# Spreading weight conversions by single steps, and moving the lead's low parts to GpSimd

## The chip, the cores and the metric

The kernel runs on one core of a Trainium2 chip. Its time is the device time of one execution in microseconds (us). TensorE (PE) multiplies matrices, VectorE (DVE), ScalarE (ACT) and GpSimd (POOL) work elementwise, and SyncE (SP) issues the transfers. Each engine takes its instructions in the order of its own queue; across engines an instruction waits on semaphores.

## The reference

```
scores = scale * q @ k^T                      # 4 batches, 8 heads, 768 tokens, 64 per head
keep   = (column < n_global) | (0 <= row - column < n_local)      # 8 and 96
a      = softmax(where(keep, scores - slope[h] * distance, -1e9))
x      = (a @ v), heads joined                # 3072 tokens x 512
h      = x @ w_in                             # 512 x 2048
out    = max(0.01 * h, h) @ w_out             # 2048 x 512
```

The weights come to the chip as float64.

## The kernel before

**Precision.** Each operand of the FFN is held as a high part in the format fp32r and a low part that is the rest, and each product is made of three matmuls: high by high, low by high, high by low (lines 797 to 799 and 818 to 820).

**Weights.** `w_in` and `w_out` come in 32 pieces; piece 2f is block f of `w_in`, piece 2f + 1 block f of `w_out`. A piece is loaded as float64 bits by the SP queue (`load_piece`, line 98, three pieces ahead, four buffers) and turned into its two parts by `split_float64` in five steps: scale (ACT, L560), shift (two DVE instructions, L563 and L565), low (DVE, L569), high (ACT, the cast L573) and rest (DVE, L576, which writes the low part). The steps depend on each other in that order, so that the piece goes back and forth between ACT and DVE. `conversion(p)` gives the first three steps to its caller and leaves high and rest in the list `due`.

**Attention.** It goes by units of one block of 128 tokens and four heads, 48 in all. `event(t)` issues the scores of unit t, the transposes of unit t - 1 (L274) and the product with v of unit t - 2 (L314, L326), and the softmax of unit t between: bias and minimum on DVE (L195), exponentials on ACT (L210), sums and reciprocals on DVE (L230, L231), and for the units below 14 a diagonal matrix `dg` on POOL (L245), by which the transposing matmul scales the rows. The high and low parts of x follow (L339 on ACT, L343 on DVE). From unit 22 on, `visit` does two units at a time.

**FFN.** Tokens go in eight chunks of 384. For each chunk there are 16 blocks f: `hidden` (called ffn1 in the text) makes block f of the hidden layer in one PSUM bank, `ps_h`; ACT copies it out (L801), DVE applies the leaky ReLU (L802), ACT casts the high part gh (L807) and DVE makes the low part gl (L808). `project` (ffn2) adds its product with `w_out` to three PSUM banks, `ps_o`, one for each 128 tokens.

**Order.** The lead is the first eight events; in events 1 to 7 pieces 0 to 6 are converted, with the steps of event t's piece between its softmax and high and rest of the piece before. After that the work goes by slots j (the loop at line 508): blocks 0 to 6 of chunk 0 are slots 0 to 6, all 16 blocks of chunk 1 are slots 7 to 22, the other blocks of chunk 0 are slots 23 to 31, and the later chunks follow. A slot issues its events (`ev_at`), then ffn1 of slot j, then ffn2 of slot j - 1. Within ffn1, `end` is called between L802 and L807 and `more` after L808. `conv_at` says which pieces a slot converts: the first in the slot's event, if there is one, the others in `more`; `end` issues what is in `due`. At slot 7, ffn2 of slot 6 ends with three ACT copies of the unfinished sums of chunk 0 (`kept`, L458), which free `ps_o` for chunk 1; a finished chunk's sums are copied by ACT, DVE, ACT (L471, L469) and written out.

Instructions that go through `pin` keep the order in which they are written on their engine. That holds for everything named up to slot 22; from slot 23 on the events below unit 22 and the slot work are not pinned, and the copies of finished chunks never are, so that the framework's planner places them.

Of the kernel before, what the change touches and what calls it, by code (L numbers as in the profile page):

```python
# [10 lines left out]
F32 = mybir.dt.float32  # L11
# [5 lines left out]
ALU = mybir.AluOpType  # L17
# [13 lines left out]
LEAD_CONV = 7  # L31
# [3 lines left out]
def spread(items, slots):  # L35

    out = {}
    for n, x in enumerate(items):
        out.setdefault(slots[n * len(slots) // len(items)], []).append(x)
    return out  # L40
# [7 lines left out]
def fast_path(ctx, tc, qp, kp, vp, wi, wo, nvec, weights, nmall, out, B, H, S):  # L48
    nc = tc.nc
# [3 lines left out]
    NF = wi.shape[0]  # L53
# [9 lines left out]
    raw = ctx.enter_context(tc.tile_pool(name="raw", bufs=2))  # L63
    att = ctx.enter_context(tc.tile_pool(name="att", bufs=2))
# [20 lines left out]
    staged = {}  # L85
# [8 lines left out]
    def load_piece(p):  # L94
        if p < len(pieces):
            m, f = pieces[p]
            t = raw.tile([P, NK * P], I64, tag="stage", name="wst", bufs=STAGES)
            pin(nc.sync.dma_start(out=t, in_=(wi, wo)[m][f].rearrange("p a b -> p (a b)")))
            staged[p] = t

    due = []

    def conversion(p):

        m, f = pieces[p]
        dh, dl = ((wih[:, :, f * P:(f + 1) * P], wil[:, :, f * P:(f + 1) * P]), (woh[:, f, :], wol[:, f, :]))[m]
        for n in range(p + 2 + (p > LEAD_CONV - 2), p + 3 + (p > LEAD_CONV - 3)):
            load_piece(n)
        scale, shift, low, *parts = split_float64(tc, pin, att, staged.pop(p), dh, dl)
        due.extend(parts)  # L110
        return scale, shift, low

# [232 lines left out]
    def event(t, conv=()):  # L345

        now, mid, old = t < NUNIT, t - 1 in units, t - 2 in units
        if t < LEAD + 2:

            av = (ps_lead if t % 2 else ps_x).tile([P, 2, 512], F32, tag="ps_av", name="ps_sc")  # L350
            scores(t, av)
            if mid and t <= LEAD:
                transposes(t - 1)
            if old:
                ov = ps_lead.tile([P, 2, 512], F32, tag="ps_ov", name="ps_ov")
                attn_v(t - 2, ov)
            if t > LEAD:

                transposes(t - 1)
        else:  # L360

            ov = av = ps_x.tile([P, 2, 512], F32, tag="ps_av", name="ps_av")
            attn_v(t - 2, ov)
            if now:
                scores(t, av)
            if mid:
                transposes(t - 1)
            high_x(t - 2, ov)
        if t + 2 < NUNIT:
            load_qk(t + 2)  # L370
        if t == 0:
            load_piece(1)
        ends = due[:]
        due.clear()
        if ends:
            ends[0]()
        scale, shift, low = conversion(conv[0]) if conv else [lambda: None] * 3
        if t + 1 < NUNIT:
            load_v(t + 1)
        scale()  # L380
        if now:
            biased(t, av)
            if t == LEAD + 1:
                high_x(t - 2, ov)
            if mid and t >= LEAD + 2:

                keep_pt(t - 1)
            exps(t)
        if t > LEAD:
            low_x(t - 2, ov)  # L390
        if ends:
            ends[1]()
        shift()
        if now:
            sums(t)
        low()
        if old and t <= LEAD:
            high_x(t - 2, ov)
        if mid and t < LEAD + 2:
            keep_pt(t - 1)  # L400
        if old and t <= LEAD:
            low_x(t - 2, ov)

    def visit(t, behind):

        ts = (t, t + 1)
        avs = [ps_x.tile([P, 2, 512], F32, tag=tag, name="ps_v") for tag in ("ps_av", "ps_t")]
        for u, av in zip(ts, avs):
            attn_v(u - 2, av)
        if t < NUNIT:  # L410
            for u, av in zip(ts, avs):
                scores(u, av)
        for u in ts:
            if u + 2 < NUNIT:
                load_qk(u + 2)
            if u + 1 < NUNIT:
                load_v(u + 1)
        for u, av in zip(ts, avs):
            high_x(u - 2, av)
        if t < NUNIT:  # L420
            biased(t, avs[0])
            exps(t)
            biased(t + 1, avs[1])
        for u, av in zip(ts, avs):
            low_x(u - 2, av)
        if t < NUNIT:
            behind.extend([lambda: exps(t + 1, [0]), lambda: (exps(t + 1, [1]), sums(t)), lambda: None, lambda: sums(t + 1)])


    half = 7  # L430
# [44 lines left out]
            eng.dma_start(out=out[r0:r0 + P, :], in_=ob)  # L475


    conv_at = {0: [7], 1: [8], 2: [9], 3: [10, 11], 4: [12], 5: [13], 6: [14]}
    conv_at.update(spread(range(15, 19), range(half, half + 4)))
    conv_at.update(spread(range(19, 2 * NF), range(half + 4, half + NF - 1)))  # L480
    ev_at = {}
    for c in range(1, NCHUNK):
        events = range(NU * first_step[c] + 2, NU * first_step[c + 1] + 2)
        slots = (range(1, half) if c == 1 else [23, 25, 26, 28, 29, 31] if c == 2 else [33, 35, 37, 40, 42, 44] if c == 3
                 else range((c - 1) * NF, c * NF - 2))
        if c > 3:

            events, slots = events[::2], [(c - 1) * NF + s for s in (2, 7, 12)]
        elif c == 3:
            events, slots = [20, 21, 22, 24], [2 * NF + s for s in (0, 3, 7, 12)]  # L490
        ev_at.update(spread(events, slots))

    for t in range(2):
# [14 lines left out]
    for j in range(len(order) + 1):  # L508
        pinned[0] = j < half + NF or bool(behind) or any(t >= PAIRS for t in ev_at.get(j, ()))
        conv = list(conv_at.get(j, ()))  # L510
        for t in ev_at.get(j, ()):
            if t >= PAIRS:
                visit(t, behind)
            else:
                event(t, conv[:1])
            conv = conv[1:]

        def end():
            for step in due:
                step()  # L520
            due.clear()
            if behind:
                behind.pop(0)()

        def more():
            if behind:
                behind.pop(0)()
            for n, p in enumerate(conv):
                if n:
                    end()  # L530
                for step in conversion(p):
                    step()
        if j == half:

            scale_bias(tc, tabs[:, 1], nbw, H, 2)
            scale_bias(tc, tabs[:, 0, HALF:], nb0, H, 2)
        if j == len(order) - NF // 4:
            band_holds(tc, fl, nvec, nmall)
        if j == len(order) - NF // 4 + 1:
            band_holds_everywhere(tc, fl, ps_x.tile([P, 2, 512], F32, tag="ps_t", name="ps_f")[0:1, 0, 0:1], flag)  # L540
        if j < len(order):
            ffn1(j, end, more)
        if j:
            ffn2(j - 1)
    return flags[0]


def split_float64(tc, pin, pool, raw, dh, dl):

    nc = tc.nc
    w2 = raw.bitcast(I32).rearrange("p (n two) -> p n two", two=2)
    lo, hi = w2[:, :, 0], w2[:, :, 1]
    w = pool.tile([P, lo.shape[1]], F32, tag="work", name="w32", bufs=2)
    wb = w.bitcast(I32)
    w3 = w.rearrange("p (a b) -> p a b", a=dh.shape[1]) if len(dh.shape) == 3 else w

    def scale():
        pin(nc.scalar.activation(out=w, in_=hi.bitcast(F32), func=AF.Copy, scale=2.0 ** -112))  # L560

    def shift():
        pin(nc.vector.tensor_scalar(out=wb, in0=wb, scalar1=3, scalar2=0x7FFFFFF8,  # L563
                                    op0=ALU.logical_shift_left, op1=ALU.bitwise_and))
        pin(nc.vector.scalar_tensor_tensor(out=wb, in0=hi, scalar=-0x80000000, in1=wb,  # L565
                                           op0=ALU.bitwise_and, op1=ALU.bitwise_or))

    def low():
        pin(nc.vector.scalar_tensor_tensor(out=wb, in0=lo, scalar=29, in1=wb,  # L569
                                           op0=ALU.logical_shift_right, op1=ALU.bitwise_or))  # L570

    def high():
        pin(nc.scalar.copy(out=dh, in_=w3))  # L573

    def rest():
        pin(nc.vector.tensor_tensor(out=dl, in0=w3, in1=dh.bitcast(F32), op=ALU.subtract))  # L576

    return scale, shift, low, high, rest

# [50 lines left out]
def scale_bias(tc, tab, nb, H, parts):  # L630
    nc = tc.nc
    for h in range(H):
        nc_scale(nc, nc.gpsimd, nb, tab, h, H, parts)
# [263 lines left out]
```

## Time and profile before

| | |
|---|---|
| median of 3 runs | 651.44 us (650.1 to 651.76) |
| profiled execution | 651.29 us, its span 649.8 us |
| PE / DVE / ACT / POOL busy | 627.9 / 375.3 / 282.2 / 22.1 us |
| mean granted TensorE clock | 0.997 |
| first FFN matmul | 37.84 us after the span's start |

A row of a timeline gives start, duration, engine, line, operation, output and inputs, shapes, count, and in brackets how long the engine stood before it and what released it. A row of waits gives the waiting engine and line, the releaser, and the wait in all, how many times, and the longest. Rows of PE with one matmul are pipelined: their starts tell more than their durations.

### The profile page before, as it was taken

What the parts mean: (1) busy time and instruction counts of PE and PEld (TensorE: products, weight loads), DVE (VectorE), ACT (ScalarE), POOL (GpSimd) and SP (SyncE); (2) the same over time, 40 slices, a digit from 0 to 9 for tenths busy, and PEclk for the clock granted to TensorE, in tenths of its full rate; (3) what the DMA queues carried; (4) which work ended last, traced back from release to release, by engine and by line L of the source; (5) the groups of instructions that cost most, each with busy time, mean ns of one, the idle gap of its engine ahead of it and who ended that gap; (6) DMA issues with size and microseconds to landing.
All of it is one profiled execution on the core that took longest, in us unless ns stands there. A gap on an engine that the chain in (4) does not pass through costs nothing.

```text
span 649.8 us, 14540 instructions
## 1 busy us (share of the span) xinstructions
PE 627.9 (97%) x5740; PEld 555.6 (86%) x5740; DVE 375.3 (58%) x1121; ACT 282.2 (43%) x796; POOL 22.1 (3%) x48
## 2 busy tenths in 40 slices
PE   6689999999999999999999999999999999999996
PEld 4478898887888888988989888989889889999985
DVE  5989978895667454553654645545645547232222
ACT  6887855554444343352442442443433524232222
POOL 3212400000000000000000000000000000000000
PEclk9899999999999999999999999999999999999999
DMA  8996634423667433343534443334343432010001
GB/s 268 321 329 202 201 128 144 145 66 121 218 204 234 135 86 115 117 155 115 174 127 153 151 116 114 131 129 152 124 132 137 159 114 98 2 49 0 2 2 52
DMA packets 55163, 88.06 MB, mean 136 GB/s; under 512 B 9776, under 2 KB 30256, under 8 KB 55088
## 3 DMA queue, kind: packets, MB, share of 16 engines
q1 hardware_dynamic: 54944, 86.79, 40.8%
q8 instruction: 47, 0.77, 0.5%
q10 hardware_dynamic: 144, 0.26, 0.1%
q14 instruction: 28, 0.23, 0.1%
HBM read 67.90 MB, written 19.14 MB: 134 GB/s over the span
## 4 chain that ended last, share of the span: by engine, by line
PE 88%; DVE 5%; ACT 4%; DMA 1%; issue 1%; POOL 0%; SPq 0%; POOLq 0%; DVEq 0%; ACTq 0%
PE ps_h L797 14%; PE ps_h L799 13%; PE ps_h L798 13%; PE ps_o L820 13%; PE ps_o L819 13%; PE ps_o L818 13%; PE ps_v L181 3%; PE ps_v L326 2%; DMA kr<-in_kp_dram 1%; PE ps_v L314 1%; ACT pr L210 1%; PE ps_av L181 1%; DVE w L569 1%; DVE w L565 1%; ACT w L560 1%
## 5 line engine op out<-in xcount | busy, mean ns | idle before, releaser
L797 PE MATMUL ps_h<-xh,wih 128*128 128x384 f32 x512 | 175.3, 342 | 0.1
L799 PE MATMUL ps_h<-xh,wil 128*128 128x384 f32 x512 | 172.1, 336 | 0.0
L798 PE MATMUL ps_h<-xl,wih 128*128 128x384 f32 x512 | 172.0, 336 | 0.0
L802 DVE SCALAR_TENSOR_TENSOR t<-t 128x384 f32<-128x384 f32 x128 | 73.8, 577 | 143.2 <-ACT t L801 141.1
L801 ACT COPY t<-ps_h 128x384 f32<-128x384 f32 x128 | 61.1, 477 | 213.3 <-PE ps_h L799 213.3
L820 PE MATMUL ps_o<-woh,gl 128*128 128x512 f32 x384 | 151.9, 396 | 0.1
L818 PE MATMUL ps_o<-woh,gh 128*128 128x512 f32 x384 | 150.7, 393 | 1.1 <-ACT part L471 0.8
L819 PE MATMUL ps_o<-wol,gh 128*128 128x512 f32 x384 | 151.1, 393 | 0.0
L797 PEld LDWEIGHTS ps_h<-xh,wih 128*128 128x128 f32 x512 | 96.1, 188 | 10.4 <-ACT xh L339 3.1
L808 DVE TENSOR_TENSOR gl<-t,gh 128x384 fp32r<-128x384 f32 x128 | 71.3, 557 | 55.1 <-ACT gh L807 55.1
L798 PEld LDWEIGHTS ps_h<-xl,wih 128*128 128x128 f32 x512 | 96.1, 188 | 4.1
L799 PEld LDWEIGHTS ps_h<-xh,wil 128*128 128x128 f32 x512 | 96.1, 188 | 0.0
L807 ACT CAST gh<-t 128x384 fp32r<-128x384 f32 x128 | 65.5, 511 | 59.4 <-DVE t L802 58.6
L820 PEld LDWEIGHTS ps_o<-woh,gl 128*128 128x128 f32 x384 | 72.2, 188 | 17.4 <-DVE gl L808 1.9
L210 ACT ACTIVATE pr<-pr,nmall 128x192 f32<-128x192 f32 (+1 forms) x192 | 83.5, 439 | 3.5 <-DVE nmall L195 2.6
L818 PEld LDWEIGHTS ps_o<-woh,gh 128*128 128x128 f32 x384 | 72.2, 188 | 13.1 <-ACT part L471 1.2
L819 PEld LDWEIGHTS ps_o<-wol,gh 128*128 128x128 f32 x384 | 72.2, 188 | 11.2
L195 DVE CUSTOM_DVE_ANT_0 pr<-ps_v,nbw 128x192 f32<-128x192 f32 x88 | 25.3, 354 | 26.2 <-ACT xh L339 26.2
L210 ACT ACTIVATION_READ_ACCUMULATOR pr<-pr,nmall 128x1 f32 x192 | 36.5, 190 | 0.0
L237 DVE TENSOR_SCALAR pr<-pr,rs 128x192 f32<-128x192 f32 (+1 forms) x136 | 33.7, 312 | 1.0
L240 DVE STREAM_TRANSPOSE pr<-pr 128x768 f32<-128x768 f32 (+1 forms) x34 | 32.1, 945 | 0.9
L339 ACT CAST xh<-ps_v 128x256 fp32r<-128x256 f32 x28 | 10.4, 373 | 38.1 <-PE ps_v L181 36.4
(94 smaller groups left out, 459.8 us busy)
## 6 DMA issues: line engine op xcount, KB each, us to landing
kr<-in_kp_dram SPq DMA_DIRECT2D x40, 384.0 KB, 4.3
vr<-in_vp_dram SPq DMA_DIRECT2D x40, 320.0 KB, 4.6
via<-pr SPq DMA_DIRECT2D x30, 384.0 KB, 2.5
pt<-via SPq DMA_DIRECT2D x120, 96.0 KB, 2.3
wst<-in_wi_dram SPq DMA_DIRECT2D x16, 512.0 KB, 4.4
wst<-in_wo_dram SPq DMA_DIRECT2D x16, 512.0 KB, 4.0
qs<-in_qp_dram SPq DMA_DIRECT2D x24, 256.0 KB, 3.5
out_dram<-part SPq DMA_DIRECT2D x20, 256.0 KB, 2.1
```

Source lines behind the costliest of these rows:

```text
L210: pin(nc.scalar.activation(out=p, in_=p, func=AF.Exp, scale=-1.0, bias=nm[:, 2 * a + j:2 * a + j + 1], accum_out=sm[:, 2 * a + j:2 * a + j ...
L237: pin(nc.vector.tensor_scalar(out=p, in0=p, scalar1=rs[:, n:n + 1], scalar2=1.0, op0=ALU.mult, op1=ALU.mult))
L797: tc.keep_in_program_order(nc.tensor.matmul(ps, lhsT=wih[:, k, fs], rhs=xh[:, k, :CT], start=(k == 0), stop=False))
L798: tc.keep_in_program_order(nc.tensor.matmul(ps, lhsT=wih[:, k, fs], rhs=xl[:, k, :CT], start=False, stop=False))
L799: tc.keep_in_program_order(nc.tensor.matmul(ps, lhsT=wil[:, k, fs], rhs=xh[:, k, :CT], start=False, stop=(k == NK - 1)))
L801: pin(copy(out=t, in_=ps))
L802: pin(nc.vector.scalar_tensor_tensor(out=t, in0=t, scalar=0.01, in1=t, op0=ALU.mult, op1=ALU.max))
L807: pin(copy(out=gh, in_=t))
L808: pin(nc.vector.tensor_tensor(out=gl, in0=t, in1=gh.bitcast(F32), op=ALU.subtract))
L818: tc.keep_in_program_order(nc.tensor.matmul(o, lhsT=gh[:, ts_], rhs=woh[:, f, :], start=first, stop=False))
L819: tc.keep_in_program_order(nc.tensor.matmul(o, lhsT=gh[:, ts_], rhs=wol[:, f, :], start=False, stop=False))
L820: tc.keep_in_program_order(nc.tensor.matmul(o, lhsT=gl[:, ts_], rhs=woh[:, f, :], start=False, stop=last))
```

## The change

Three things are changed.

1. In the lead, the rest step of pieces 0 to 5 is done by POOL instead of DVE. Later pieces keep DVE.
2. No piece is converted in slot 0. Pieces 7 to 14 go to slots 1 to 6; the slots with two pieces are 4 (10 and 11) and 6 (13 and 14), where before it was slot 3 (10 and 11).
3. Pieces 15 to 31 are no longer placed whole. Their 85 steps form one stream in the order scale, shift, low, high, rest of piece 15, then of piece 16, and so on, and slots 7 to 21 take five or six steps each: two in `end` (none in slot 7) and the others in `more`. Before, one piece was converted in each of these slots and two in slots 11 and 16, with scale, shift and low in `more` and high and rest in the next `end`.

Along with it, the event of unit 14 moves from slot 23 to 24, those of units 16 and 18 by a slot too, and the events of units 20 and 21 from slots 32 and 35 to 33 and 36.

```diff
-        scale, shift, low, *parts = split_float64(tc, pin, att, staged.pop(p), dh, dl)
+        scale, shift, low, *parts = split_float64(tc, pin, att, staged.pop(p), dh, dl,
+                                                  nc.gpsimd if p < LEAD_CONV - 1 else nc.vector)
...
-    conv_at = {0: [7], 1: [8], 2: [9], 3: [10, 11], 4: [12], 5: [13], 6: [14]}
-    conv_at.update(spread(range(15, 19), range(half, half + 4)))
-    conv_at.update(spread(range(19, 2 * NF), range(half + 4, half + NF - 1)))
+    conv_at = {1: [7], 2: [8], 3: [9], 4: [10, 11], 5: [12], 6: [13, 14]}
+    steps_at = [len(x) for x in spread(range(5 * (2 * NF - 15)), range(half, half + NF - 1)).values()]
+
+    def stream():
+
+        for p in range(15, 2 * NF):
+            steps = conversion(p)
+            parts = due[-2:]
+            del due[-2:]
+            yield from steps
+            yield from parts
+
+    coming = stream()
...
-        slots = (range(1, half) if c == 1 else [23, 25, 26, 28, 29, 31] if c == 2 else [33, 35, 37, 40, 42, 44] if c == 3
+        slots = (range(1, half) if c == 1 else [24, 25, 27, 28, 30, 31] if c == 2 else [33, 35, 37, 40, 42, 44] if c == 3
...
-            events, slots = [20, 21, 22, 24], [2 * NF + s for s in (0, 3, 7, 12)]
+            events, slots = [20, 21, 22, 24], [2 * NF + s for s in (1, 4, 7, 12)]
...
             due.clear()
+            if 0 < j - half < NF - 1:
+                for _ in range(2):
+                    next(coming)()
...
                 for step in conversion(p):
                     step()
+            if 0 <= j - half < NF - 1:
+                for _ in range(steps_at[j - half] - 2 * (j > half)):
+                    next(coming)()
...
-        pin(nc.vector.tensor_tensor(out=dl, in0=w3, in1=dh.bitcast(F32), op=ALU.subtract))
+        pin(low_engine.tensor_tensor(out=dl, in0=w3, in1=dh.bitcast(F32), op=ALU.subtract))
```

More of the change, by code (lines that the diff above doesn't have):

```diff
@@ L545, in fast_path, with split_float64 @@
     return flags[0]
-def split_float64(tc, pin, pool, raw, dh, dl):
+def split_float64(tc, pin, pool, raw, dh, dl, low_engine):
     nc = tc.nc
```

## The prediction

> **What bounds the kernel now.** I began with the page, for the engines' shares.
>
> ```profile
> span 649.8 us, 14540 instructions
> PE 627.9 (97%) x5740; PEld 555.6 (86%) x5740; DVE 375.3 (58%) x1121; ACT 282.2 (43%) x796; POOL 22.1 (3%) x48
> ```
>
> TensorE is the bound behind the lead, so a gain must come from places where it stands still, or from the lead, where it has little to do. Next, TensorE's waits between 37 and 200 us (in all, times, longest):
>
> ```profile
> PE ps_tr L274 <- POOL dg L245: 2.2, 2, 1.4
> PE ps_o L818 <- ACT part L471: 0.8, 1, 0.8
> PE ps_o L818 <- ACT gh L807: 0.4, 2, 0.2
> ```
>
> Three kinds of stall, and little else: this is all that better placing can win there. Then the timeline of each engine at these places. For the first kind, TensorE and ScalarE around FFN slots 1 to 3:
>
> ```profile
> 40.12 0.45 PE L314 MATMUL ps_av<-pt,vr 64*64 64x128 f32 x8
> 47.40 0.83 PE L181 MATMUL ps_av<-kr,qs 64*64 64x192 f32 x16
> 49.62 0.93 PE L274 MATMUL ps_tr<-dg,pr 64*64 64x64 f32 x48 [1.39 <-POOL dg L245]
> ...
> 54.84 0.45 PE L314 MATMUL ps_av<-pt,vr 64*64 64x128 f32 x8
> 55.58 0.83 PE L181 MATMUL ps_av<-kr,qs 64*64 64x192 f32 x16
> 56.23 0.88 PE L274 MATMUL ps_tr<-dg,pr 64*64 64x64 f32 x48
> ```
>
> ```profile
> 44.39 0.62 ACT L573 CAST woh<-w 128x512 fp32r<-128x512 f32 x1 [1.69 <-DVE w L569]
> 46.17 0.45 ACT L210 ACTIVATE pr<-pr,nmall 128x192 f32<-128x192 f32 x1
> ...
> 57.99 0.46 ACT L210 ACTIVATE pr<-pr,nmall 128x192 f32<-128x192 f32 x1
> ```
>
> In a good slot the exponentials (L210) begin 57.99 - 54.84 = 3.15 us after the slot's first attention matmul; in slot 1 it is 46.17 - 40.12 = 6.05, because piece 7's cast, queued ahead of them on ScalarE, waits 1.69 us for VectorE (L569). L274 then starts 49.62 - 47.40 = 2.22 us behind L181 instead of 56.23 - 55.58 = 0.65: 1.57 lost.
>
> The second chunk (slots 7 to 22) decides this case. Its rhythm on TensorE, and what a slot takes where two pieces fall into one:
>
> ```profile
> 81.39 0.34 PE L797 MATMUL ps_h<-xh,wih 128*128 128x384 f32 x1
> 85.54 0.34 PE L797 MATMUL ps_h<-xh,wih 128*128 128x384 f32 x1
> ...
> 106.27 0.34 PE L797 MATMUL ps_h<-xh,wih 128*128 128x384 f32 x1
> 111.23 0.34 PE L797 MATMUL ps_h<-xh,wih 128*128 128x384 f32 x1
> ```
>
> A slot is 85.54 - 81.39 = 4.15 us; the one after the pair of pieces 19 and 20 takes 4.96, so 0.8 is lost, and the waits on gh above say that this happens twice: 1.6 us.
>
> How the conversions fit between is seen on VectorE and ScalarE just behind that pair:
>
> ```profile
> 111.16 0.55 DVE L802 SCALAR_TENSOR_TENSOR t<-t 128x384 f32<-128x384 f32 x1
> 111.92 0.69 DVE L576 TENSOR_TENSOR wol<-w,woh 128x512 fp32r<-128x512 f32 x1 [0.22 <-ACT woh L573]
> 112.53 0.55 DVE L808 TENSOR_TENSOR gl<-t,gh 128x384 fp32r<-128x384 f32 x1
> 113.00 0.42 DVE L563 TENSOR_SCALAR w<-w 128x512 int32<-128x512 int32 x1
> 113.46 0.69 DVE L565 SCALAR_TENSOR_TENSOR w<-wst,w 128x512 int32<-128x512 int32 x1
> 114.18 0.69 DVE L569 SCALAR_TENSOR_TENSOR w<-wst,w 128x512 int32<-128x512 int32 x1
> 114.79 0.55 DVE L802 SCALAR_TENSOR_TENSOR t<-t 128x384 f32<-128x384 f32 x1
> ```
>
> ```profile
> 111.27 0.62 ACT L573 CAST woh<-w 128x512 fp32r<-128x512 f32 x1 [1.66 <-DVE w L569]
> 111.80 0.51 ACT L807 CAST gh<-t 128x384 fp32r<-128x384 f32 x1
> ...
> 113.57 0.48 ACT L801 COPY t<-ps_h 128x384 f32<-128x384 f32 x1 [0.68 <-PE ps_h L799]
> ```
>
> With one piece per slot, low (L569) is a slot's last step and the cast (L573) comes behind the next slot's copy L801: the copy never waits for low. A cycle behind a backlog is 114.79 - 111.16 = 3.63 us, under 4.15, so a backlog melts.
>
> **The change, part by part.** The sum is made against the profiled execution, 651.29 us (span 649.8 and 1.5 around it), 0.15 below the median of 651.44.
>
> *Slot 0 empty.* Slot 1's exponentials then start up to 2.9 us earlier, more than the 1.57 that was lost: **-1.6**. Slot 3's pair (pieces 10, 11) moves to slot 4, and the other L274 stall (0.8 of the 2.2) should move along: 0, between -0.8 and +0.8. Piece 14 becomes the second piece of slot 6; its price stands in the next part but one.
>
> *Pool takes the low parts of pieces 0 to 5.* One event of the lead, and what Pool does elsewhere:
>
> ```profile
> 17.79 0.62 ACT L573 CAST woh<-w 128x512 fp32r<-128x512 f32 x1 [0.64 <-DVE w L569]
> 19.11 0.69 DVE L576 TENSOR_TENSOR wol<-w,woh 128x512 fp32r<-128x512 f32 x1
> 20.57 0.19 ACT L210 ACTIVATION_READ_ACCUMULATOR pr<-pr,nmall 128x1 f32 x1
> 20.86 0.17 DVE L230 TENSOR_SCALAR rs<-sm 128x4 f32<-128x4 f32 x1
> ```
>
> ```profile
> 9.85 0.61 POOL L245 TENSOR_TENSOR dg<-eye,rs 128x256 f32<-128x256 f32 x1
> 60.52 0.88 POOL L245 TENSOR_TENSOR dg<-eye,rs 128x256 f32<-128x256 f32 x1 [1.56 <-DVE rs L231]
> 60.83 0.97 DVE L802 SCALAR_TENSOR_TENSOR t<-t 128x384 f32<-128x384 f32 x1
> ```
>
> L576 leaves VectorE (0.6 us each), but L230 waits for the exponentials too, which end at 20.57 + 0.19 = 20.76, so an event gains at most 20.86 - 20.76 = 0.10; six events, 0.6. No row shows Pool at 128x512: twice the 128x256 product is 1.22 to 1.76 us. VectorE loses time beside Pool: L802 takes 0.97 instead of 0.55 and ends 0.4 after Pool's row does. If L563 is held likewise, it starts when Pool ends: 17.79 + 0.62 + 1.22 = 19.63, against 19.72 today (19.11 + 0.61), or 20.17, 0.45 late, five times over. Pool is free, and dg, behind the subtraction in its queue, comes only after L230. Between 0.6 gained and 2.3 lost, near the free-running 0.61 row: **-0.3**.
>
> The Trainium skill (GPSIMD Engine Reference, 4.1 Engine selection) speaks against this part: elementwise work on a tile belongs on VectorE, GpSimd being about twice as slow on two inputs. Its 4497 ns for 2048 elements (section 3.1) makes an estimate of 1.1 us here; by that the part is a gain of some 0.4 instead of 0.3. The rows agree with the ratio (0.61 for 256 elements, against 0.69 for 512 on VectorE).
>
> *The second chunk by steps.* Write S, H, L, C, R for scale (ScalarE), shift (L563, L565), low (L569), cast (ScalarE) and rest (L576). The stream issues, ahead of | before gh and behind it after gl: slot 7 |S15 H15 L15 C15 R15 S16; 8 H16 L16|C16 R16 S17 H17; 9 L17 C17|R17 S18 H18; 10 L18 C18|R18 S19 H19 L19; 11 C19 R19|S20 H20 L20 C20; 12 R20 S21|H21 L21 C21; 13 R21 S22|H22 L22 C22 R22, and so on, 5 or 6 a slot. As many instructions as before; but now C often follows its own L, and ScalarE's queue, in order, stands until VectorE is done. Behind C in that queue stand gh, L801 and the copies that free ps_o. The copies come first:
>
> ```profile
> 85.25 0.67 ACT L560 ACTIVATE w<-wst 128x512 f32<-128x512 f32 x1
> 85.83 1.53 ACT L458 COPY kept<-ps_o 128x512 f32<-128x512 f32 x3
> ...
> 87.62 0.39 PE L818 MATMUL ps_o<-woh,gh 128*128 128x512 f32 x1
> ```
>
> Today only S15 is ahead of the kept copies. Then all of piece 15 is, and S16. Counted from 81.39, the start of slot 7's first matmul, with gl of slot 6 at +1.0 as now: slot 6's second piece 14 has H at 1.5, L at 2.7, C at 3.4; gh of slot 7 follows at 4.0, R14 4.1, gl 4.7, H15 5.2, L15 6.4, C15 7.1, S16 7.6, kept 8.2, done by 8.8. TensorE wants the bank at 87.62 - 81.39 = 6.2: a stall of 2.6. If slot 6 runs 0.7 late behind the moved stall, 3.3. I take **+3.0**.
>
> From slot 8 on I step the queues by start distances read off the rows above: L801 to L802 0.51, L802 to the next 0.52, L576 0.61, L808 0.47, L563 0.46, L565 0.72, L569 to C 0.72, C to the next on ScalarE 0.53, C to L576 0.65; ffn1 of the next slot needs L801 done (1.3 us of slack), ffn2 needs gh (2.2). Slot 12 shows the mechanism, from its L801 to the next: 0.51 + 0.52 + R20 0.61 + gl 0.47 + 0.46 + 0.72 + L21 0.72 + C21 0.53 = 4.54, not 3.63: 0.4 over TensorE's slot, each time C ends a slot. Where a backlog from H and L of the slot before meets it (slots 10 to 11, 18 to 19), a cycle is 6 us and more. Stepped through, TensorE stands 0.5, 0.4, 0.1, 1.2, 0.4, 0.4, 1.0 (slots 10 to 16), 0.7 (18, 19) and 1.1 (21, 22): **+5.7**. The same stepping of the old order gives 0.65 twice, where the trace has 0.8. The bounds: 0, if ScalarE's slack takes all of it, and 7.5, if each stop also costs some 0.15 of restarting, the amount by which the stepping falls short. The pairs' stalls go: **-1.6**. Loads are issued at S, three pieces ahead as before, behind no new wait.
>
> *Events 14 and 20 later by a slot.*
>
> ```profile
> 159.36 0.58 ACT L471 COPY part<-ps_o 128x512 f32<-128x512 f32 x1
> ...
> 159.99 0.50 PE L818 MATMUL ps_o<-woh,gh 128*128 128x512 f32 x1 [0.78 <-ACT part L471]
> ```
>
> The third output copy of chunk 1, late between event 14's work, holds TensorE 0.8, 1.0 with restarts. Without the event in slot 23 nothing but slot work stands around it: **-1.0**; 0 if the scheduler, free there, puts it last again.
>
> Sum: -1.6 - 0.3 + 3.0 + 5.7 - 1.6 - 1.0 = +4.2, 655.5 against 651.3; with the median's 0.15, **655.6**.
>
> **The rivals.** (1) *The stalls go and no wait takes their place*: faster. It needs ScalarE to lose nothing by standing at C, that is, C's L must end before gh, L801 or a copy is wanted. For it: ScalarE is busy 43% of the span, and the slack of 1.3 and 2.2 us a slot. Against it: the 1.66 us that C waited for L569 at 111.27, with gh right behind. Time: 651.4 - 1.6 - 0.3 - 1.6 - 1.0 = 646.9. It decides once a cycle stays under 4.15 us and kept starts before 87.6. (2) *Only the kept copies stall*, and the cycles melt as now: 646.9 + 3.0 = 649.9. For it: 4.54 is over 4.15 by little, and the slack could carry a few. Against it: over a dozen slots it is used up. (3) *Pool holds VectorE in the lead* 0.45 us five times: 655.6 + 0.3 + 2.3 = 658.2. For it: the 0.97 row; against: free-running 0.61. (4) *Pool relieves nothing*, the exponentials being the end of an event: 655.9, inside the forecast's own range.
>
> **How the numbers follow.** A measurement here tells about 0.3% (2 us) from no change. Forecast with (4): 0.55, own range 653.4 to 657.5. (3): 0.10. (2): 0.13, of which half lies within 0.3%. (1): 0.22. Slower 0.64, same 0.11, faster 0.25, with some of the forecast's lower tail counted as same. The range reaches from 647.0, where half of (1) is left out, to 659.0.
>
> **What would show it.** Right: in slot 7 the L458 rows start some 2.5 us later against slot 8's L797, and TensorE shows an L818 waiting for kept; ScalarE's L573 waits for L569 in sum over well more than now, L797 then waits for L801 in slots 13 to 16 and 21; L274's wait on dg at slot 2 is gone; the part stall is gone; L576 on POOL near 1.2 us. Wrong: slots of 4.15 us throughout the second chunk, or kept copies that come ahead of C15; either leaves only the gains.

## The result and the profile after

The changed kernel takes **655.05 us** (median of 12 runs, 653.44 to 658.27), beside 650.51 us for the kernel before on the same chip (12 runs, 649.21 to 651.76): a ratio of 1.0068, 95% interval 1.0054 to 1.0081. It is slower by 4.5 us; 655.6 was predicted. The profiled execution is 654.65 us, its span 653.1, at a mean granted clock of 0.996.

In the changed kernel the lines of the attention are one further on (L458 is L459, L471 is L472), those of the conversion and the FFN seventeen: scale L577, shift L580 and L582, low L586, cast L590, rest L593, the FFN's copy L818, gh L824, gl L825, ffn1 L814 to L816, ffn2 L835 to L837. The page of the changed kernel:

```profile
span 653.1 us, 14532 instructions
PE 629.2 (96%) x5740; PEld 555.7 (85%) x5740; DVE 373.1 (57%) x1115; ACT 282.8 (43%) x796; POOL 29.8 (5%) x54
```

Six instructions have gone from VectorE to Pool. Neither VectorE nor ScalarE has more instructions than before; the time was lost in the order. The waits of all engines between 37 and 200 us (in all, times, longest), after:

```profile
ACT woh L590 <- DVE w L586: 19.4, 13, 2.4
ACT wih L590 <- DVE w L586: 17.5, 12, 2.4
...
PEld ps_h L814 <- ACT t L818: 3.9, 6, 0.9
...
PE ps_o L835 <- ACT kept L459: 2.8, 1, 2.8
...
PE ps_tr L275 <- POOL dg L246: 0.9, 1, 0.9
PE ps_h L814 <- ACT t L818: 0.8, 2, 0.4
```

And two rows of the same view of the kernel before:

```profile
ACT woh L573 <- DVE w L569: 12.5, 10, 1.9
...
ACT wih L573 <- DVE w L569: 7.9, 8, 1.6
```

ScalarE stands at the cast, waiting for low, 36.9 us instead of 20.4. Two waits of TensorE are new: ffn2 for the kept copies, and ffn1 for ScalarE's copy of the hidden block. Two are gone: ffn2 for the part copy and for gh. Of the two on `dg`, 2.2 us in all, one is left, 0.9, the one that moved along with the pair of pieces 10 and 11.

**The kept copies.** ScalarE's timeline in slot 8, after:

```profile
85.80 0.62 ACT L590 CAST woh<-w 128x512 fp32r<-128x512 f32 x1 [2.03 <-DVE w L586]
86.33 0.66 ACT L577 ACTIVATE w<-wst 128x512 f32<-128x512 f32 x1
86.90 1.54 ACT L459 COPY kept<-ps_o 128x512 f32<-128x512 f32 x3
88.32 0.50 ACT L818 COPY t<-ps_h 128x384 f32<-128x384 f32 x1
```

The cast of piece 15 and the scale of piece 16 stand ahead of the copies, as the order was read; the copies begin 4.45 us after slot 8's first ffn1 matmul (82.45), where before it was 0.29 (85.83 - 85.54). TensorE at the same place:

```profile
82.45 0.34 PE L814 MATMUL ps_h<-xh,wih 128*128 128x384 f32 x1
...
84.40 0.34 PE L816 MATMUL ps_h<-xh,wil 128*128 128x384 f32 x1
87.51 0.77 PE L835 MATMUL ps_o<-woh,gh 128*128 128x512 f32 x1 [2.78 <-ACT kept L459]
88.08 0.63 PE L836 MATMUL ps_o<-wol,gh 128*128 128x512 f32 x1
88.51 0.63 PE L837 MATMUL ps_o<-woh,gl 128*128 128x512 f32 x1
88.93 0.63 PE L835 MATMUL ps_o<-woh,gh 128*128 128x512 f32 x1
...
91.27 0.34 PE L814 MATMUL ps_h<-xh,wih 128*128 128x384 f32 x1
```

ffn2 is late by 87.51 - (84.40 + 0.17) = 2.94 us; 0.17 is the distance between the starts of two ffn1 matmuls. Then comes something the prediction did not have: its matmuls start 0.43 us apart instead of 0.23. The view by stretches (us, busy time and matmuls of PE, granted clock, DMA share, GB/s), after:

```profile
84.50:87.50 3.00, 0.23 (x2) 1.00 0.45 126
87.50:91.20 3.70, 3.69 (x9) 0.54 0.29 111
```

and before, at the same time:

```profile
87.50:91.20 3.70, 3.70 (x20) 1.00 0.47 144
```

The granted clock was 0.54 for 3.7 us behind the stall. Slot 8 takes 91.27 - 82.45 = 8.82 us instead of 4.14; 2.94 of the 4.68 is the stall, 1.74 the slow clock.

**The cycles.** The end of slot 12 on the three engines, after:

```profile
106.62 0.69 DVE L586 SCALAR_TENSOR_TENSOR w<-wst,w 128x512 int32<-128x512 int32 x1
107.34 0.62 ACT L590 CAST wih<-w 128x512 fp32r<-128x512 f32 x1 [2.03 <-DVE w L586]
107.62 0.40 PE L837 MATMUL ps_o<-woh,gl 128*128 128x512 f32 x1
107.87 0.47 ACT L818 COPY t<-ps_h 128x384 f32<-128x384 f32 x1
108.39 0.45 PE L814 MATMUL ps_h<-xh,wih 128*128 128x384 f32 x1 [0.38 <-ACT t L818]
```

Low of piece 21 goes from 106.62, its cast from 107.34, the copy behind it from 107.87, and ffn1, ready 0.23 after 107.62, begins at 108.39: 0.54 late. This is the mechanism that was stepped through.

To see where the time goes, the start of each slot (its first ffn1 matmul on TensorE's timeline) is set against the one of the kernel before:

| stretch | predicted | measured |
|---|---|---|
| up to slot 1 (lead) | -0.3 | -1.50 |
| slots 1 to 2 (slot 0 empty) | -1.6 | -1.63 |
| slots 2 to 8 (the pair that moves) | 0 | +0.04 |
| slot 8: kept | +3.0 | +2.94 |
| slot 8: clock | none | +1.74 |
| slots 9 to 22: cycles and pairs | +5.7 - 1.6 = +4.1 | +1.96 |
| slots 22 to 25 (part copy) | -1.0 | -1.04 |
| slots 25 to 34 | 0 | +0.81 |
| sum | +4.2 | +3.3 |

The spans differ by the same 3.3 us (653.1 - 649.8), the medians by 4.5. The row of the lead differs by as much between profiles whose lead is the same (see Pool below); without it the rows add up to 4.8.

### The profile page after: what moved, and what is told of

It reads as the page before. It is cut to its first block, busy times and chain, and to the rows that moved or that the text cites. A ratio compares the mean times of both kernels' runs of the same rounds, so it can differ in the third digit from the quotient of the medians.

```text
span 653.1 us, 14532 instructions
## 1 busy us (share of the span) xinstructions
PE 629.2 (96%) x5740; PEld 555.7 (85%) x5740; DVE 373.1 (57%) x1115; ACT 282.8 (43%) x796; POOL 29.8 (5%) x54
## 4 chain that ended last, share of the span: by engine, by line
PE 80%; DVE 10%; ACT 3%; issue 3%; DMA 3%; SPq 0%; POOL 0%; DVEq 0%; ACTq 0%; POOLq 0%
PE ps_h L814 12%; PE ps_o L837 12%; PE ps_h L816 12%; PE ps_h L815 12%; PE ps_o L836 12%; PE ps_o L835 12%; PE ps_v L182 3%; DVE w L586 2%; DVE w L582 2%; PE ps_v L327 2%; DVE w L580 2%; PE ps_v L315 1%; DMA kr<-in_kp_dram 1%; PE ps_av L182 1%; DVE t L819 1%
## 5 line engine op out<-in xcount | busy, mean ns | idle before, releaser
L814 PE MATMUL ps_h<-xh,wih 128*128 128x384 f32 x512 | 176.0, 344 | 1.3 <-ACT t L818 0.8
L816 PE MATMUL ps_h<-xh,wil 128*128 128x384 f32 x512 | 172.1, 336 | 0.0
L835 PE MATMUL ps_o<-woh,gh 128*128 128x512 f32 x384 | 151.3, 394 | 2.8 <-ACT kept L459 2.8
L837 PE MATMUL ps_o<-woh,gl 128*128 128x512 f32 x384 | 152.3, 397 | 0.0
L818 ACT COPY t<-ps_h 128x384 f32<-128x384 f32 x128 | 61.2, 478 | 198.9 <-PE ps_h L816 198.8
L814 PEld LDWEIGHTS ps_h<-xh,wih 128*128 128x128 f32 x512 | 96.0, 188 | 13.9 <-ACT t L818 3.9
L825 DVE TENSOR_TENSOR gl<-t,gh 128x384 fp32r<-128x384 f32 x128 | 71.3, 557 | 57.6 <-ACT gh L824 57.6
L816 PEld LDWEIGHTS ps_h<-xh,wil 128*128 128x128 f32 x512 | 96.0, 188 | 0.1
L824 ACT CAST gh<-t 128x384 fp32r<-128x384 f32 x128 | 65.5, 512 | 60.9 <-DVE t L819 60.6
L837 PEld LDWEIGHTS ps_o<-woh,gl 128*128 128x128 f32 x384 | 72.6, 189 | 16.9 <-DVE gl L825 1.2
L835 PEld LDWEIGHTS ps_o<-woh,gh 128*128 128x128 f32 x384 | 72.5, 189 | 14.4 <-ACT kept L459 3.1
```

Source lines behind the costliest of these rows:

```text
L814: tc.keep_in_program_order(nc.tensor.matmul(ps, lhsT=wih[:, k, fs], rhs=xh[:, k, :CT], start=(k == 0), stop=False))
L816: tc.keep_in_program_order(nc.tensor.matmul(ps, lhsT=wil[:, k, fs], rhs=xh[:, k, :CT], start=False, stop=(k == NK - 1)))
L818: pin(copy(out=t, in_=ps))
L824: pin(copy(out=gh, in_=t))
L825: pin(nc.vector.tensor_tensor(out=gl, in0=t, in1=gh.bitcast(F32), op=ALU.subtract))
L835: tc.keep_in_program_order(nc.tensor.matmul(o, lhsT=gh[:, ts_], rhs=woh[:, f, :], start=first, stop=False))
```

## The experiments

Theory A is the prediction's: ScalarE takes its queue in order, so a cast placed right behind its own low stands until VectorE is done, and the kept copies, the copy of the hidden block and gh stand behind it. Against it stood, in the expectations, that Pool's subtraction or the new slots of pieces 7 to 14 cost the time (rival B), that the steps simply load VectorE too much (rival C), and that Pool wins 2.2 us in the lead by relieving VectorE (rival D). Unless said otherwise, an experiment is the changed kernel with the edit shown; `plan_more` and `plan_end` list the steps (piece, step) that a slot issues behind gl and ahead of gh.

**Without the stream.** Pieces 15 to 31 whole, as before; the lead, the empty slot 0 and the events as in the change.

```diff
-    steps_at = [len(x) for x in spread(range(5 * (2 * NF - 15)), range(half, half + NF - 1)).values()]
...
+    plan_end, plan_more = {}, {}
+    at = {7: [15], 8: [16], 9: [17], 10: [18]}
+    at.update(spread(range(19, 2 * NF), range(half + 4, half + NF - 1)))
+    for j, ps in at.items():
+        for n, p in enumerate(ps):
+            plan_more.setdefault(j, []).extend((p, k) for k in range(3))
+            (plan_more if n + 1 < len(ps) else plan_end).setdefault(j + (n + 1 == len(ps)), []).extend([(p, 3), (p, 4)])
...
-    coming = stream()
...
```

> The changed kernel, but pieces 15 to 31 placed whole, as before the change (two of them in slots 11 and 16); the lead, slot 0 and the moved events stay changed. Theory A (ScalarE stands at a cast that was issued right behind its own low step, and the kept copies and L801 stand behind it): the 4.7 us of slot 8 and the 2.0 net of slots 9 to 22 go, so 655.05 - 6.7 = 648.3 us, faster than before by some 2 us; no TensorE wait for kept, and the two pair stalls of 0.8 us are back. Rival B (the Pool subtraction or the other slots of pieces 7 to 14 cost the time): 653 us or more, as the changed kernel.

Measured: 647.52 us (12 runs) beside 649.54 (26 runs), ratio 0.9964 (0.9949 to 0.998). Slots 8 to 22 run as in the kernel before, to 0.1 us. The stream is what costs the time, and rival B falls; the rest of the change is a gain of 2 us.

**The stream alone.** The lead on VectorE, slots 0 to 6 and the events as before; only the stream is new.

```diff
-                                                  nc.gpsimd if p < LEAD_CONV - 1 else nc.vector)
+                                                  nc.vector)
...
-    conv_at = {1: [7], 2: [8], 3: [9], 4: [10, 11], 5: [12], 6: [13, 14]}
+    conv_at = {0: [7], 1: [8], 2: [9], 3: [10, 11], 4: [12], 5: [13], 6: [14]}
...
-[24, 25, 27, 28, 30, 31]
+[23, 25, 26, 28, 29, 31]
...
-for s in (1, 4, 7, 12)]
+for s in (0, 3, 7, 12)]
```

> The kernel before with the stream of single steps in slots 7 to 21 and nothing else: low parts of the lead on VectorE, pieces 7 to 14 and the events where they were. Theory A: the kept copies come 2.0 to 2.6 us late and the cycles with a standing cast cost 3.5 to 5.7 us, less the 1.6 of the pairs: +4 to +7, 654.5 to 657.5 us. Rival B: no more than before, 650.5 us.

Measured: 655.04 us (6 runs), ratio 1.0078 (1.0052 to 1.0104). Slot 8 is longer than before by 2.1 us, slots 9 to 22 by 3.0. ffn2 of slot 8 waits for the copies here too, less long, since slot 6 holds one piece and not two:

```profile
87.43 0.50 PE L835 MATMUL ps_o<-woh,gh 128*128 128x512 f32 x1 [1.80 <-ACT kept L459]
87.76 0.39 PE L836 MATMUL ps_o<-wol,gh 128*128 128x512 f32 x1
87.99 0.39 PE L837 MATMUL ps_o<-woh,gl 128*128 128x512 f32 x1
```

The clock stays full. With the pair in slot 6 the stall is 1 us longer, and in the profile of the change the slow clock came with it.

**The kept copies first, and a little earlier.** The stream stays; only where it is cut changes (`steps_at` is written out as numbers here, the first line being the change's). In the first kernel slot 7 takes scale, shift and low of piece 15 alone, and slot 8 nine steps; in the second only the scale of piece 16 moves from slot 7 to 8.

```diff
-    steps_at = [6, 6, 5, 6, 6, 5, 6, 6, 5, 6, 6, 5, 6, 6, 5]
+    steps_at = [3, 9, 5, 6, 6, 5, 6, 6, 5, 6, 6, 5, 6, 6, 5]
```

```diff
-    steps_at = [6, 6, 5, 6, 6, 5, 6, 6, 5, 6, 6, 5, 6, 6, 5]
+    steps_at = [5, 7, 5, 6, 6, 5, 6, 6, 5, 6, 6, 5, 6, 6, 5]
```

> The changed kernel, but slot 7 takes only scale, shift and low of piece 15, and slot 8 nine steps; from slot 9 on the steps stand where they stood. Theory A: the kept copies follow S15 directly, so the stall of 2.9 us in slot 8 goes, and with it the 1.7 us in which TensorE ran its matmuls at 0.43 us instead of 0.23 behind that stall; the cycles with a standing cast stay. 655.05 - 4.6 = 650.5 us, up to 1.3 more where the later steps of slot 8 stand closer. If the slots' rhythm and not the kept copies make the loss, 654 us or more.

> The changed kernel, but S16 goes from slot 7 to slot 8, so that the kept copies start 0.57 us earlier and the stall in slot 8 is 2.4 us instead of 2.9. If TensorE's slow matmuls behind the stall come from the length of the stall and 2.4 us is below what sets them off, the slow stretch goes too: the first matmul of slot 9 comes 2.3 us earlier, 652.7 us in all. If they come from any stall, only 0.57 is won, 654.5 us, and the slow 0.43 us spacing is still there.

Measured: 651.51 us (10 runs), ratio 1.0038 (1.0019 to 1.0057), and 653.74 us (5 runs), ratio 1.006 (1.0035 to 1.0084). In the first, slot 8 is 4.17 us long: no stall and no slow clock. But slots 9 to 22 now lose 4.3 us instead of 2.0, with three steps more behind slot 8's gl than in the change. In the second the wait is shorter (2.38 us counted as above), and the slow clock is still there: slot 8 takes 8.06 us.

**Steps, but no cast behind its own low.** As the kernel with the kept copies first, but a cast that would follow its own low in one group of steps is put off to the next group (`end` or `more`), with its rest.

```diff
+    carried = []
+    for j in range(half, half + NF):
+        for plan in (plan_end, plan_more):
+            items, carried = carried + plan.get(j, []), []
+            plan[j] = []
+            for p, k in items:
+                late = (k == 3 and (p, 2) in plan[j]) or (k == 4 and (p, 3) in carried)
+                (carried if late else plan[j]).append((p, k))
...
```

> As kept_early, with the same steps in the same slots, except that a cast that would stand in one group with its own low step (ahead of gh, or behind gl) is issued at the head of the next group, and its rest step with it. The work and the slots' loads are the same; only the place of about ten casts in ScalarE's queue differs. Theory A (the cycles are long because ScalarE stands at these casts): the 5.9 us that slots 9 to 22 of kept_early take beyond 4.15 us each shrink to 0.2 by the stepping of the queues, 651.5 - 5.7 = 645.8 us. Rival C (VectorE's own work of 5 or 6 steps a slot is too much, whatever the order): 650 to 651.5 us.

Measured: 645.1 us (8 runs) beside 649.75 (19 runs), ratio 0.9925 (0.9899 to 0.995): faster than both kernels. ScalarE's waits between 80 and 160 us fall accordingly:

```profile
ACT woh L602 <- DVE w L598: 6.2, 8, 1.3
ACT wih L602 <- DVE w L598: 5.0, 5, 1.9
```

in the changed kernel they are, in the same stretch,

```profile
ACT woh L590 <- DVE w L586: 15.6, 9, 2.4
ACT wih L590 <- DVE w L586: 15.3, 9, 2.4
```

TensorE's matmuls have no wait left on kept, on the copy of the hidden block or on gh. VectorE has the same instructions to do, and from 86 to 150 us it is busy 55.6 us, more than the 50.1 of the changed kernel, while TensorE never stands; so its load is not what held the changed kernel, and rival C falls. The rest steps move along with the casts, and what their place alone is worth was not measured. Spreading by steps is no loss in itself: with the casts apart even the two stalls behind pairs, 1.7 us, are gone.

**Whole pieces, with the second of a pair spread over two slots.** In slots 10 and 16, scale and shift of a second piece, its low in the next slot's `end`, cast and rest in its `more`.

```diff
...
+        if j in (10, 16):
+            plan_more[j].extend([(p, 0), (p, 1)])
+            plan_end[j + 1].append((p, 2))
+            plan_more.setdefault(j + 1, []).extend([(p, 3), (p, 4)])
+            p += 1
...
```

> The changed kernel with pieces 15 to 31 whole (cast and rest at the head of the next slot), except that the second piece of a pair is spread over two slots: scale and shift behind the first piece in slot 10 or 16, low at the end step of the next slot, cast and rest ahead of that slot's own piece. Theory A: no cast stands in front of gh or L801, and the two pair stalls of whole_pieces (0.8 us each) go as well: 647.5 - 1.6 = 645.9 us, faster than both kernels. If the pairs' stalls come from VectorE's sum of work in two slots, 647.5 us.

Measured: 645.65 us (6 runs), ratio 0.9933 (0.9917 to 0.9949), with no wait of TensorE's matmuls on ScalarE left in slots 9 to 22. Two ways of keeping casts away from their lows reach the same time.

**Pool.** Two kernels: the kernel before with the low parts of the lead on Pool and nothing else, and the changed kernel with them on VectorE.

```diff
-        scale, shift, low, *parts = split_float64(tc, pin, att, staged.pop(p), dh, dl)
+        scale, shift, low, *parts = split_float64(tc, pin, att, staged.pop(p), dh, dl,
+                                                  nc.gpsimd if p < LEAD_CONV - 1 else nc.vector)
...
-        pin(nc.vector.tensor_tensor(out=dl, in0=w3, in1=dh.bitcast(F32), op=ALU.subtract))
+        pin(low_engine.tensor_tensor(out=dl, in0=w3, in1=dh.bitcast(F32), op=ALU.subtract))
```

```diff
-                                                  nc.gpsimd if p < LEAD_CONV - 1 else nc.vector)
+                                                  nc.vector)
```

> The kernel before with the low parts of pieces 0 to 5 made by Pool, nothing else. The forecast had -0.3 us for it (at most -0.6); the changed kernel's first FFN matmul came 2.2 us earlier. Theory A: Pool's part is small, 0.3 to 0.8 us, and the other 1.5 us come from where a stall without a releaser ('issue') falls in the lead: the time lies within 1 us of before, 649 to 650.5, and the first FFN matmul between 35.5 and 37.5 us. Rival D (Pool relieves VectorE by 2.2 us): the first FFN matmul at 35.6 us, and the kernel faster by 2 us.

> The changed kernel with the low parts of pieces 0 to 5 back on VectorE, all else as changed. Theory A: the first FFN matmul still at 35.5 to 36.5 us, and the time as the changed kernel's within 1 us, 654 to 656 us. Rival D: the first FFN matmul at 37.8 us and 657 us.

Measured: 649.39 us (10 runs), ratio 0.9995 (0.9982 to 1.0009), and 654.43 us (4 runs), ratio 1.0067 (1.0047 to 1.0087), as the changed kernel. Pool neither gains nor costs anything that can be told; rival D falls. The start of slot 0, though, missed what was expected of it: 38.65 us in the second kernel. With Pool in the lead it lies between 34.98 and 36.80 us (seven profiles), without it between 35.52 and 38.65 (seven profiles). Among what differs there are waits of TensorE that the profile puts down to nothing ("issue"); between 24 and 38 us the changed kernel shows

```profile
PE ps_ov L327 <- issue: 0.6, 1, 0.6
```

and the same kernel with the lead on VectorE

```profile
PE ps_tr L275 <- issue: 2.3, 1, 2.3
```

That kernel brought a second surprise. It has the stall of the changed kernel at the same instruction:

```profile
86.66 0.33 PE L816 MATMUL ps_h<-xh,wil 128*128 128x384 f32 x1
89.81 0.50 PE L835 MATMUL ps_o<-woh,gh 128*128 128x512 f32 x1 [2.82 <-ACT kept L459]
90.15 0.39 PE L836 MATMUL ps_o<-wol,gh 128*128 128x512 f32 x1
90.38 0.40 PE L837 MATMUL ps_o<-woh,gl 128*128 128x512 f32 x1
```

ffn2 is late by 2.98 us, and the clock stays full: 0.23 us between matmuls.

**The clock behind a stall.** Four kernels measure this by itself: the kernel before, with ScalarE copying the first bank of kept n times more than once, n = 5 to 8.

```diff
-                pin(nc.scalar.copy(out=kept[-1], in_=o[tt]))
+                for _ in range(n + 1 if tt == 0 else 1):
+                    pin(nc.scalar.copy(out=kept[-1], in_=o[tt]))
```

> The kernel before, with ScalarE copying the first bank of kept five times more ahead of the three copies. A copy is 0.51 us and the first copy of the changed kernel freed its bank 0.61 after it began, so TensorE stands 85.83 + 0.61 + 5 x 0.51 - 87.62 = 1.4 us in slot 8. Theory A (the clock halves after an idle time between 1.97 and 2.38 us, counted as the time by which the start of ffn2 is late): full spacing of 0.23 us behind it, slot 8 of 4.15 + 1.4 = 5.55 us. Rival (what decides is where the stall falls in time, not its length): the spacing may be 0.43 here.

> Six copies more: the start of ffn2 in slot 8 is late by 1.9 us. Theory A: still full spacing (1.97 left it at full speed in the kernel with the stream alone), slot 8 of 6.05 us. Rival: 0.43 behind it is possible.

> Seven copies more: late by 2.4 us. Theory A: spacing of 0.43 us for some 3 us behind it, as after the 2.38 us with scale of piece 16 moved, slot 8 of 4.15 + 2.4 + 1.3 = 7.85 us, the time 3.7 above the kernel before. Rival: full spacing is possible, 6.55 us.

> Eight copies more: late by 2.9 us, as in the changed kernel. Theory A: spacing of 0.43 us, slot 8 of 4.15 + 2.9 + 1.7 = 8.75 us, the time 4.6 above the kernel before. Rival: full spacing is possible, 7.05 us.

Copies of one bank into one tile follow each other in 0.61 us, not 0.51, so the stalls are longer than planned. Slow means starts 0.43 us apart in ffn2, 0.32 in ffn1. (The before of these four: 649.36 us, 14 runs.)

| kernel | ffn2 late by | slow stretch | time | ratio (95%) |
|---|---|---|---|---|
| n = 5 | 1.92 | none | 651.41 | 1.0032 (1.0015 to 1.0048) |
| n = 6 | 2.54 | 3.4 us from 89.6 | 654.71 | 1.0072 (1.005 to 1.0094) |
| n = 7 | 3.16 | 3.4 us from 90.9 | 654.39 | 1.0079 (1.0056 to 1.0102) |
| n = 8 | 3.75 | 3.4 us from 90.5 | 654.1 | 1.0076 (1.0053 to 1.0099) |

Each slow stretch begins up to 1.5 us after the stall has ended, lasts 3.4 us and costs 1.7, whatever the stall's length. The times do not rise from n = 6 to 8 although the stalls do; with four or five runs each, and intervals of about 1.5 us either way, they cannot tell. Length alone, by which Theory A of these expectations reckoned, does not decide: between 2.38 and 3.75 us five stalls were followed by a slow stretch and one, of 2.98 us in the kernel with the lead on VectorE, was not. That speaks for the rival, that it matters where in time the stall falls.

The traces show how. Within one execution the granted clock changes only at whole multiples of 3.413 us from its other changes: in the changed kernel's profile it rises at 15.90, falls at 87.58, which is 21.0 such windows later, and rises again one window on, at 90.99. This holds in all 14 profiles; where the windows begin differs from profile to profile. Cut along its own windows, a stall can be judged by TensorE's busy time in each (columns as above). The changed kernel:

```profile
84.16:87.58 3.42, 0.64 (x5) 1.00 0.49 149
87.58:90.99 3.41, 3.41 (x8) 0.50 0.30 118
```

the kernel with the lead on VectorE:

```profile
85.08:88.50 3.42, 1.91 (x11) 1.00 0.49 153
88.50:91.91 3.41, 2.10 (x9) 1.00 0.52 159
```

and n = 7:

```profile
84.02:87.44 3.42, 2.38 (x14) 1.00 0.00 0
87.44:90.85 3.41, 1.47 (x6) 1.00 0.50 154
90.85:94.26 3.41, 3.41 (x11) 0.50 0.02 5
```

The changed kernel's stall of 2.94 us lies in one window, which is busy for 0.64 of 3.42 us, and the next window has half the clock. The stall of 2.98 us is shared by two windows, busy for 1.91 and 2.10, and both are followed by full clock. Over the eight stalls in slot 8, half clock followed the windows that were busy for 19 to 43% of their length, and never one that was busy for 56% or more. In the leads of the 14 profiles the same holds for windows at full clock, but between 46 and 49% they went either way.

**The stall and the cycles together.** How much longer than before the stretches are, in us, and how this adds up, with -1.6 for the empty slot 0 and -1.0 for the moved event where a kernel has them, to the times measured (difference of the medians):

| kernel | slot 8 | slots 9 to 22 | both | sum | measured |
|---|---|---|---|---|---|
| the change | +4.68 | +1.96 | +6.6 | +4.0 | +4.5 |
| lead on VectorE | +3.12 | +2.99 | +6.1 | +3.5 | +4.7 |
| kept a little earlier | +3.92 | +2.14 | +6.1 | +3.5 | +4.2 |
| stream alone | +2.08 | +3.00 | +5.1 | +5.1 | +5.5 |
| kept first | +0.03 | +4.30 | +4.3 | +1.7 | +2.0 |
| whole pieces | +0.03 | +0.04 | +0.1 | -2.5 | -2.0 |
| pairs split | +0.01 | -1.18 | -1.2 | -3.8 | -4.1 |
| casts apart | +0.01 | -1.71 | -1.7 | -4.3 | -4.65 |

The sums leave out the lead and what lies behind slot 25, where the profiles differ from the kernel before by up to 1.8 us either way even in slots 34 to 127, which no edit but the moved events touches; and still they come within 0.7 of the measured times in all rows but one, where it is 1.2 (whose interval is 1.3 either way).

## Why the prediction was right, and where it was not

**The direction and the mechanism.** The likeliest case came true: ScalarE's queue stands at casts that follow their own low. Rival (1), that no wait takes the place of the stalls, and rival (2), that only the kept copies stall, are both refuted by the slots; with the kept copies first, 4.3 us are still lost in slots 9 to 22. What rival (1) asked for, low done before its cast is wanted, is what the kernel with the casts apart arranges, and that one gives 645.1.

**Slot 0 empty, -1.6:** -1.63 by this row, but slots 0 and 1 have to be read together. They take 12.6 to 12.9 us in the seven profiles with piece 7 in slot 0, also where slot 1's stall on `dg` is missing, because an "issue" wait of 1.0 to 1.6 us in slot 0 stands in its place (the stream alone, Pool alone, n = 6 and 8). With slot 0 empty they take 11.0 us in four profiles, which is the gain forecast, 11.7 in the changed kernel's own, and 12.8 and 13.1 with the casts apart and the pairs split, where such a wait, 1.6 and 1.8 us, takes the gain away. **The pair that moves, 0:** +0.04; the wait on `dg` moved to slot 6's event, as forecast. **The event at slot 24, -1.0:** -1.04, and no wait on the part copy is left.

**The kept copies, +3.0:** 2.94, between the 2.6 of the queue alone and the 3.3 with a late slot 6. Counting the ScalarE queue ahead of the copies was right; the sign named for it, copies that start some 2.5 us later against slot 8, was not what that count gives (8.2 - 4.15 - 0.29 = 3.8), and they start 4.45 - 0.29 = 4.16 us later. What failed is what was left out behind it: the sum charged a stall with its length alone, and in the profiled execution the halved clock added 1.74. Not every execution has to have it: in the lead-on-VectorE profile the same stall falls across two windows.

**The cycles, +5.7 with -1.6 for the pairs:** 1.96 net instead of 4.1. (The single stalls listed there, 18 and 19 as well as 21 and 22 taken together, add up to 5.8.) The stepping of the queues was right in kind (slot 12's cycle is 0.54 over TensorE's slot, forecast 0.4; slots 13 to 17, 19, 21 and 22 start 0.4 to 0.6 late, forecast were 13 to 16, 21 and others). The stalls of 0.5 and 0.4 in slots 10 and 11 did not come, and those of 1.2 and 1.0 in slots 13 and 16 came as 0.54 and 0.40. The step that failed is adding this term and the kept copies' as if they were independent. While TensorE stands in slot 8, ScalarE and VectorE work off their backlog, and slots 9 to 11 then lose nothing. The cleanest pair for this is the changed kernel and the one with the lead on VectorE: the same steps in the same slots and the same stall, but 1.56 us more in slot 8 by the slow clock. Slots 9 to 22 then take 1.03 us less, nearly all of it in slots 10 to 12. With the copies first, so that slot 8 gives no such time, slots 9 to 22 lose 4.30 net, close to the 4.1 of the stepping, but there slot 8 also takes nine steps instead of six, and what that adds was not measured apart. Over all rows of the table, whose steps differ, more time in slot 8 goes with less behind it.

**Pool, -0.3:** not to be told from nothing. The parts can be seen in the lead, after:

```profile
12.72 0.88 POOL L246 TENSOR_TENSOR dg<-eye,rs 128x256 f32<-128x256 f32 x1 [2.28 <-DVE rs L232]
...
16.78 0.88 POOL L246 TENSOR_TENSOR dg<-eye,rs 128x256 f32<-128x256 f32 x1 [1.65 <-DVE rs L232]
17.22 0.62 ACT L590 CAST woh<-w 128x512 fp32r<-128x512 f32 x1 [0.32 <-DVE w L586]
17.92 1.28 POOL L593 TENSOR_TENSOR wol<-w,woh 128x512 fp32r<-128x512 f32 x1 [0.26 <-ACT woh L590]
18.54 0.94 DVE L580 TENSOR_SCALAR w<-w 128x512 int32<-128x512 int32 x1
19.52 0.69 DVE L582 SCALAR_TENSOR_TENSOR w<-wst,w 128x512 int32<-128x512 int32 x1
20.78 0.88 POOL L246 TENSOR_TENSOR dg<-eye,rs 128x256 f32<-128x256 f32 x1 [1.58 <-DVE rs L232]
```

and Pool's rows of the same events before:

```profile
12.97 0.88 POOL L245 TENSOR_TENSOR dg<-eye,rs 128x256 f32<-128x256 f32 x1 [2.51 <-DVE rs L231]
17.34 0.88 POOL L245 TENSOR_TENSOR dg<-eye,rs 128x256 f32<-128x256 f32 x1 [3.50 <-DVE rs L231]
21.41 0.88 POOL L245 TENSOR_TENSOR dg<-eye,rs 128x256 f32<-128x256 f32 x1 [3.19 <-DVE rs L231]
```

Pool takes 1.28 us (1.22 to 1.76 were estimated) and VectorE's L580 beside it 0.94 instead of 0.42, ending just behind Pool: it is held, as rival (3) had it. But L582 then begins 19.52 - 17.22 = 2.30 us after the cast, against 20.17 - 17.79 = 2.38 before, so no event is late; this event takes 20.78 - 16.78 = 4.00 us instead of 4.07. The event ahead of it gains more, 16.78 - 12.72 = 4.06 instead of 17.34 - 12.97 = 4.37, more than the 0.10 that the prediction held to be the most; the other profiles agree (4.06 to 4.26 with Pool, 4.37 to 5.03 without). With three events like this one that makes 0.5, which is less than the times of the whole kernel can tell. The estimate of 1.1 us for this subtraction by the Trainium skill (GPSIMD Engine Reference, 3.1) was short by 0.2; going against its rule of section 4.1, elementwise work on VectorE, cost nothing that can be told here (ratio 0.9995).

**What makes the sum come out.** The table's lead row, -1.50, was not foreseen; some 0.5 of it can be Pool's, by the rows above, and the rest is not the change's by any run here. The +0.81 in slots 25 to 34 comes in slot 33's event, where a transfer is late in this execution:

```profile
205.25 0.85 PE L315 MATMUL ps_av<-pt,vr 64*64 64x128 f32 x5 [0.48 <-DMA pt<-via]
```

Of the other profiles with the same events, four (whole pieces, kept first, casts apart, lead on VectorE) gain 0.25 there from slot 31 to 34, the one with the pairs split 0.14, and the one with kept a little earlier loses 0.86 by the same late transfer. So 655.6 came close partly because a missing term (the clock) and one too large (the cycles) offset each other.

## What to carry to other kernels

When work that goes back and forth between two in-order engines is spread more finely, look at which instruction stands right behind its own producer: the queue behind it stands too, and the cure is not fewer steps but a step in another slot. Do not add up stalls along one chain as if each stood alone; time that the bound engine stands in one place lets the others catch up, and of 1.56 us that the slow clock took in slot 8, 1.03 came back in the slots behind it. And a stall of TensorE of 2.4 us or more may cost 1.7 us more than its length, or not, by where it falls in time.

## What was not expected of the hardware

The granted clock fell to half after TensorE had stood for 2.38 to 3.75 us, in five of six such stalls, and not after 1.92 and 1.97; the slow stretch lasted 3.4 us each time. What decided was how much of a single 3.41 us window the stall took: half clock came when TensorE was busy for 43% of a window or less, not when it was for 56% or more. The Trainium skill (TensorE: Matmul & The Clock Gate, Part 1) describes half rate after an idle window of about 3.4 us, with windows that run freely, and full rate again after a busy one. The 3.4 us of the slow stretches agree with it, and so does a stall of 2.98 us that passed without effect; that a stall of 2.38 us, shorter than a window, was enough differs from its wording. Where between 43 and 56% the limit lies, these stalls do not show, and in the leads windows busy for 46 to 49% went either way.

Where TensorE's "issue" waits of 0.4 to 2.3 us in the lead fall changes from kernel to kernel, also where nothing of the lead was edited: the four kernels with repeated copies, whose lead is that of the kernel before, start slot 0 at 35.70 to 37.44 us, and it at 37.84. The slow clock goes along with it: the five profiles with a stretch of half clock that begins behind 26 us start slot 0 at 36.48 to 38.65, the other nine at 34.98 to 36.48. Which of the two brings the other is open, and so is where the "issue" waits come from. A single profile's lead is therefore no evidence for a term below about 2 us.
